# Linear-attention recurrence: state update and output in fp32, with the inverse and the output scores on block diagonals

## The chip, the cores and the metric

The kernel runs on one NeuronCore of a Trainium2 chip. The metric is the device time of one execution in microseconds; the number that counts is the median over several executions. In the profile PE is TensorE's matmul side and PEld its weight loads, DVE is VectorE, ACT is ScalarE, POOL is GpSimd and SP is SyncE, which issues most DMAs.

## The reference

Three stages follow each other: a delta-rule attention, a mixture of experts with one expert for each token, and a gated MLP. The change touches the first stage alone:

```python
# batch 4, heads 8, sequence 768, head size 48, all float32
k_n = k / (norm(k, axis=-1) + 1e-6)
state = zeros((B, H, D, D))
for t in range(S):
    y[:, :, t] = q_t @ state
    v_old = state.T @ k_t
    state = state + beta_t * outer(k_t, v_t - v_old)
x = y.transpose(0, 2, 1, 3).reshape(B * S, H * D)     # 3072 tokens x 384
x = moe(x)      # gate by argmax, 8 experts, relu(x @ w1) @ w2
x = mlp(x)      # (sigmoid(x @ w_gate) * (x @ w_val)) @ w_out
```

## The kernel before

**Stages.** Attention fills about the first 380 us of the span, the experts the next 200 and the MLP the rest. Only attention has recurrence, and only attention is changed.

**Tiling.** The sequence is cut into 24 chunks of 32 tokens (a "step" `s`). A step has 8 heads x 4 batches = 32 independent small problems. Batch `b` owns the partitions `quad(b)` = 32b to 32b+31 of each token-major tile, and its 48 state rows sit on one half of the partitions (`rows(b)`). So nearly each matmul of the loop is a small one, issued 32 times over (h, b); a matmul in fp32 shows as two MATMUL records with two weight loads in the trace, one in fp16 as one.

**One step of the main loop.** `KS` = K x state (32 fp32 matmuls). `W` = values minus `KS` (DVE). `Y` starts with Q x state (32 fp32). `U` = T x `W` (32 fp32), where T (`XTS`) is the inverse of a unit triangular 32x32 matrix per (h, b). ACT and DVE then split `U` into a high and a low fp16 half, `UH`. The state `Sps` grows in PSUM by K-transposed x U: three passes of 32 fp16 matmuls (high x high, low x high, high x low: `PASS`), with `KHG` the fp16 halves of K scaled by its inverse lengths. ACT copies the state to `SH` for the next step. `Y` gets P x U, again three passes of 32 fp16 matmuls with `PHL`, the masked scores K x Q in fp16 halves. Between these stand, on the PE, three 128x128 transposes of the step before (`XTP`), the gate's logits (`GL`) and the products K x [K, Q] of the chunk eleven steps ahead (`GP`, 24 of 32 before the state update and 8 at the step's end, in steps 1 to 12).

**Work beside it.** ACT scales the raw K of the next pair of chunks (`kh_mul`: 8 small activations a step) and makes the high halves; POOL makes the low halves (`kh_split_lo`, `p_split_lo`), scales and masks P (`p_split`), scales V (`v_mul`) and half of the triangular matrices (`scale`). DVE forms T column by column for a group of four chunks (`inv_ops`: pairs of multiply into `tmp` and add into `X`, then one transpose into `XTS`), several steps ahead; `Filler` deals these out in pieces of a fixed modelled length (`TA`, `TB`) between the step's own DVE work.

**What sets the order.** Each engine has a `Queue` that issues strictly in program order, so that an instruction that waits holds all behind it on its engine. SP's queue holds the loads of K and Q (`load_kq`), of K and V by token (`load_kth`, `load_v`) and the zeroing of the dispatch buffer (`zero_fill`).

Of the kernel before, what the change touches and what calls it, by code (L numbers as in the profile page):

```python
# [31 lines left out]
SIG, KSC = 1024.0, 64.0  # L32
# [107 lines left out]
class Attention:  # L140
# [5 lines left out]
    def run(self, small, acc, zero_fill, small_loads):  # L146
# [17 lines left out]
        rnt = cp.tile([128, NG, 32], F32, name="rnt")  # L164
# [79 lines left out]
        def p_evac(s):  # L244
            u, s2 = divmod(s, 2)
            ps = PP.pop(s)
            for h in range(8):
                A.activation(out=PM[u][:, 8 * s2 + h], in_=ps[:, h, 0:32], func=AF.Copy, scale=rnt[:, 0, 8 * s + h : 8 * s + h + 1])

        def gp_evac(s):  # L250

            ps = GPS.pop(s)
            g, s4 = divmod(s, 4)
            if s4 == 0 and g > 0:
                GPM[g] = [ep.tile([128, 32, 32], F32, tag=n, name=n, bufs=b) for n, b in (("G", 2), ("P", 2))]
            A.copy(out=GPM[g][0][:, 8 * s4 : 8 * s4 + 8], in_=ps[:, :, 0:32])
            return A.copy(out=GPM[g][1][:, 8 * s4 : 8 * s4 + 8], in_=ps[:, :, 32:64]).ins


        PMS = {}  # L260

        def p_split(u):
            g, i = divmod(u, 2)
            if g:
                pm = GPM[g][1][:, 16 * i : 16 * i + 16]
                G.tensor_tensor(out=pm, in0=pm, in1=rnt[:, g, 16 * i : 16 * i + 16].unsqueeze(2).to_broadcast([128, 16, 32]), op=ALU.mult)
            else:
                pm = PM.pop(u)
            G.tensor_tensor(out=pm, in0=pm, in1=mask.unsqueeze(1).to_broadcast([128, 16, 32]), op=ALU.mult)
            PHL[u] = wk.tile([128, 2, 16, 32], F16, tag="PHL", name="PHL", bufs=4)  # L270
            PMS[u] = pm

        def p_split_hi(u):
            A.copy(out=PHL[u][:, 0], in_=PMS[u])

        def p_split_lo(u):
            G.tensor_tensor(out=PHL[u][:, 1], in0=PMS.pop(u), in1=PHL[u][:, 0], op=ALU.subtract)

        def kh_mul(u, half=None):
            r = rnt[:, u // 2].rearrange("p (s h) -> p s h", s=4)  # L280
            for i in (range(2) if half is None else (half,)):
                kt = KTOK[u][:, i]
                if u == 0 or KA:
                    for h in range(8):
                        A.activation(out=kt[:, :, h], in_=kt[:, :, h], func=AF.Copy, scale=r[:, 2 * (u % 2) + i, h : h + 1])
                    continue
                G.tensor_tensor(out=kt, in0=kt, in1=r[:, 2 * (u % 2) + i].unsqueeze(1).to_broadcast([128, 48, 8]), op=ALU.mult)

        by_head = lambda x: x.rearrange("p d h -> p h d")

        def kh_split_hi(u):
            KH = wk.tile([128, 2, 2, 8, 48], F16, tag="KH", name="KH", bufs=2)
            for s in range(2):
                A.copy(out=KH[:, s, 0], in_=by_head(KTOK[u][:, s]))
            KHG[u] = KH

        def kh_split_lo(u):
            KH, src = KHG[u], KTOK.pop(u)
            for s in range(2):
                G.tensor_tensor(out=KH[:, s, 1], in0=by_head(src[:, s]), in1=KH[:, s, 0], op=ALU.subtract)  # L300


        def prep(g):
# [4 lines left out]
            R = R0 if g < 2 else R2  # L308
# [5 lines left out]
            def scale(E, j0, j1, i0):  # L314
                L = Lt[:, j0:j1, i0:]
                E.tensor_tensor(out=L, in0=L, in1=x[:, j0:j1].unsqueeze(2).to_broadcast([128, j1 - j0, 32 - i0]), op=ALU.mult)
                E.tensor_tensor(out=L, in0=L, in1=nbr[:, g, i0:].unsqueeze(1).to_broadcast([128, j1 - j0, 32 - i0]), op=ALU.mult)
# [26 lines left out]
        others = []  # L344
# [7 lines left out]
        def inv_ops(g, share=32):  # L352
# [53 lines left out]
            def last(F):  # L406
# [4 lines left out]
                F.done = g  # L411
                if g == 0:
# [15 lines left out]
        def x_evac(s, Yp):  # L428
# [3 lines left out]
            A.activation(out=XG[s][:, 0:384], in_=fl(Yp), func=AF.Copy, scale=1.0 / SIG)  # L432
# [10 lines left out]
        def gate_l(s, mm=None):  # L443
# [140 lines left out]
        GPM[0] = [ep.tile([128, 32, 32], F32, tag="G", name="G", bufs=2)]  # L584
# [8 lines left out]
        G.tensor_copy(out=lt, in_=small["tri"])  # L593
        for ops in prep(0):
# [46 lines left out]
        kh_mul(1)  # L641
        kh_split_hi(1)
# [4 lines left out]
        p_split_lo(0)  # L647
# [784 lines left out]
```

## Time and profile before

| | before |
|---|---|
| median of 3 runs | 1108.39 us (1106.78 to 1110.62) |
| the profiled execution | 1108.68 us, its span 1107.0 us |
| PE busy over the span | 983.4 us, 89% |
| DVE, ACT, POOL busy | 553.9, 386.6, 408.0 us |
| mean granted TensorE clock | 0.864 of full speed |

The span runs from the first to the last instruction; 1.7 us of the execution lie around it. [...] Matmul records overlap each other, so the time that a stream takes is read from its union, not from the length of one record. "issue" is idle time for which the profile shows no semaphore.

### The profile page before, as it was taken

To read this page: it belongs to the slowest core of one execution; us is meant where nothing else is said; L and a number is where in the kernel's file an instruction comes from. 1 tells how busy PE (TensorE), PEld (TensorE's weight loads), DVE (VectorE), ACT (ScalarE), POOL (GpSimd) and SP (SyncE) were. 2 spreads that over 40 slices of the span, in tenths; PEclk is the share of its full clock that TensorE was granted. 3 is DMA by queue.
4 is the path that set the end of the run, shared out by engine and by line. 5 is a ranking of instruction groups with operands and counts; after the bars stand their busy time and mean duration, and the time that the engine had idled before them with its cause. 6 is when DMAs were issued, how large, how long until landed. Compare 5 with 4: busy or idle time off the path is not lost. (4 is left out here: it accounts for less than half of the span.)

```text
span 1107.0 us, 34055 instructions
## 1 busy us (share of the span) xinstructions
PE 983.4 (89%) x15079; PEld 869.3 (79%) x15080; DVE 553.9 (50%) x1338; ACT 386.6 (35%) x848; POOL 408.0 (37%) x439
## 2 busy tenths in 40 slices
PE   7966677776766899999899999999999999999997
PEld 6955666665655798889788988888888888888886
DVE  5987698879842357777665355421211201210111
ACT  2642444444442244545445522221211211211111
POOL 3652455555622224445434423341231322312322
PEclk7965666566555599999999999999999999999999
DMA  8434322211132255555554222100000000000000
GB/s 214 115 119 118 90 75 76 72 51 47 46 104 61 75 175 166 168 168 159 159 148 134 76 59 72 44 29 1 1 29 1 15 15 1 29 1 1 29 1 29
DMA packets 49866, 82.16 MB, mean 74 GB/s; under 512 B 7193, under 2 KB 37154, under 8 KB 49714
## 3 DMA queue, kind: packets, MB, share of 16 engines
q1 hardware_dynamic: 46642, 70.48, 21.9%
q0 software_dynamic: 3072, 9.46, 2.3%
q8 instruction: 119, 1.95, 0.8%
q14 instruction: 33, 0.27, 0.1%
HBM read 64.13 MB, written 15.80 MB: 72 GB/s over the span
## 5 line engine op out<-in xcount | busy, mean ns | idle before, releaser
L1353 DVE TENSOR_TENSOR gf<-gf,g 128x512 f32<-128x512 f32 x72 | 49.5, 688 | 309.0 <-PE g L1345 308.5
L855 POOL TENSOR_TENSOR gsl<-gf,gsh 128x512 fp32r<-128x512 f32 x68 | 88.4, 1300 | 268.7 <-ACT gsh L854 268.7
L1352 ACT ACTIVATE gf<-g 128x512 f32<-128x512 f32 x72 | 43.0, 598 | 185.1 <-PE g L1345 182.4
L86 DVE TENSOR_TENSOR tmp<-X,Lt 128x60 f32<-128x60 f32 (+33 forms) x280 | 97.5, 374 | 2.0
L86 DVE TENSOR_TENSOR X<-X,tmp 128x60 f32<-128x60 f32 (+33 forms) x280 | 96.6, 370 | 1.2
L854 ACT CAST gsh<-gf 128x512 fp32r<-128x512 f32 x69 | 42.8, 620 | 145.2 <-DVE gf L1353 144.6
L1319 PE MATMUL o<-woh,gsl 128*128 128x384 f32 x272 | 87.2, 338 | 0.0
L1319 PE MATMUL o<-wol,gsh 128*128 128x384 f32 x272 | 86.5, 337 | 0.0
L1035 DVE SCALAR_TENSOR_TENSOR hl<-h,hh 128x460 fp32r<-128x460 f32 (+7 forms) x57 | 33.1, 581 | 61.6 <-ACT hh L1034 61.4
L994 PE MATMUL y<-hh,w2h 128*128 128x460 f32 (+6 forms) x168 | 60.9, 362 | 2.3 <-ACT hh L1034 2.2
L1345 PE MATMUL g<-yl,wgh 128*128 128x512 f32 x216 | 62.6, 395 | 0.0
L1345 PE MATMUL g<-yl,wvh 128*128 128x512 f32 x216 | 62.3, 395 | 0.0
L1319 PE MATMUL o<-woh,gsh 128*128 128x384 f32 x272 | 61.7, 337 | 0.0
L1345 PE MATMUL g<-yh,wgh 128*128 128x512 f32 x180 | 60.9, 395 | 0.0
L994 PE MATMUL y<-hh,w2l 128*128 128x460 f32 (+6 forms) x168 | 58.5, 348 | 0.0
L86 ACT ACTIVATE kth<-kth,rnt 128x48 f32<-128x48 f32 x192 | 54.7, 388 | 1.6 <-DMA kth<-in_ktok_dram 1.6
L86 PE MATMUL Y<-UH,PHL 32*32 32x48 f16 x2304 | 29.2, 201 | 28.9 <-issue 28.9
L1319 PEld LDWEIGHTS o<-woh,gsh 128*128 128x128 f32 x272 | 49.7, 188 | 5.8
L86 PE MATMUL Sps<-UH,KH 32*48 32x48 f16 x2208 | 28.3, 200 | 27.4 <-issue 16.1
L1319 PEld LDWEIGHTS o<-wol,gsh 128*128 128x128 f32 x272 | 50.6, 188 | 2.4
L1345 PE MATMUL g<-yh,wgl 128*128 128x512 f32 x180 | 51.9, 395 | 0.0
L1345 PE MATMUL g<-yh,wvh 128*128 128x512 f32 x180 | 51.7, 395 | 0.0
(318 smaller groups left out, 2331.4 us busy)
## 6 DMA issues: line engine op xcount, KB each, us to landing
w1r<-in_w_dram SPq DMA_DIRECT2D x32, 384.0 KB, 4.9
w2r<-in_w_dram SPq DMA_DIRECT2D x32, 384.0 KB, 3.6
KQ<-in_st_dram SPq DMA_DIRECT2D x40, 192.0 KB, 4.3
disp<-zrow SPq DMA_DIRECT2D x8, 772.0 KB, 7.0
kth<-in_ktok_dram SPq DMA_DIRECT2D x12, 384.0 KB, 3.6
VT<-in_vtok_dram SPq DMA_DIRECT2D x12, 384.0 KB
XG<-in_m2g_dram SPq DMA_DIRECT2D x12, 384.0 KB, 5.0
XG<-in_m2v_dram SPq DMA_DIRECT2D x12, 384.0 KB, 4.3
```

What stands on the lines that cost most here:

```text
L86: r = f(*args, **kw)
L854: (act or nc.scalar).copy(out=hi, in_=src)
L855: eng.tensor_tensor(out=lo, in0=src, in1=hi, op=ALU.subtract)
L994: self.T.matmul(out=ys[c][:, 0:n], lhsT=w2[l][:, f % 2, 128 * c : 128 * c + 128], rhs=(hh, hl)[r], start=(f == 0 and i == 0), stop=(f == 7 ...
L1035: self.V.scalar_tensor_tensor(out=hl, in0=hp[:, 0:n], scalar=0.0, in1=hh, op0=ALU.max, op1=ALU.subtract)
L1319: T.matmul(out=ops_[m][:, 0:384], lhsT=gh[l][:, 128 * m : 128 * m + 128], rhs=wo[r][:, f], start=(f == 0 and i == 0), stop=(f == 11 and i ...
L1345: T.matmul(out=ps, lhsT=gv[w][l][:, c, 128 * f : 128 * f + 128], rhs=Y[r][c], start=(i == 0 and c == 0), stop=(i == 2 and c == 2))
L1352: A.activation(out=gf, in_=gps[0], func=AF.Sigmoid)
L1353: V.tensor_tensor(out=gf, in0=gf, in1=gps[1], op=ALU.mult)
```

## The change

Lengths of K are no longer multiplied into K and P; they go into the scale of the inverse's rows (`nbr` is multiplied by the inverse length a second time), so U comes out scaled for raw K and raw P. The state update is one fp32 pass on the loaded K tile (`KTOK`), the output is 8 fp32 matmuls of 128x128, one a head, on P laid out as a block diagonal over the four batches (`PBD`); from the second group on `U` is 16 matmuls of 64x64 on T laid out as a two-block diagonal (`TBD`). DMAs of SP scatter T and P into these, whose other blocks are zeroed once. V is scaled on ACT, P is masked on DVE as it leaves PSUM (on POOL for the first 12 chunks), and the triangular matrices are scaled on DVE alone. The logits take three full matmuls instead of six halves.

```diff
+        PM = [cp.tile([128, 8, 32], F32, name=f"PM{i}") for i in range(RK)]
+        PBD = [cp.tile([128, 8, 4, 32], F32, name=f"PBD{i}") for i in range(2)]
+        TBD = [cp.tile([128, 32, 2, 32], F32, name=f"TBD{i}") for i in range(2)]
...
-            t = wk.tile([128, 2, 48, 8], F32, tag="kth", name="kth", bufs=1)
+            t = wk.tile([128, 2, 48, 8], F32, tag="kth", name="kth", bufs=3)
...
-            v = VT[s // 2][:, s % 2].rearrange("p (h e) -> p h e", h=8)
-            G.tensor_tensor(out=v, in0=v, in1=nt[:, g, 8 * s4 : 8 * s4 + 8].unsqueeze(2).to_broadcast([128, 8, 48]), op=ALU.mult)
+            for h in range(8):
+                v = VT[s // 2][:, s % 2, 48 * h : 48 * h + 48]
+                A.activation(out=v, in_=v, func=AF.Copy, scale=nt[:, g, 8 * s4 + h : 8 * s4 + h + 1])
...
+        def p_keep(s, ps):
+
+            A.copy(out=PM[s % RK], in_=ps)
+            G.tensor_tensor(out=PM[s % RK], in0=PM[s % RK], in1=mask.unsqueeze(1).to_broadcast([128, 8, 32]), op=ALU.mult)
...
+        def p_evac(s):
+            V.tensor_tensor(out=PM[s % RK], in0=GPS.pop(s)[:, :, 32:64], in1=mask.unsqueeze(1).to_broadcast([128, 8, 32]), op=ALU.mult)
+
+        def p_expand(s):
+            for b in range(4):
+                SP.dma_start(out=PBD[s % 2][quad(b), :, b], in_=PM[s % RK][quad(b)])
+
+        def t_expand(g):
+            for b in range(4):
+                SP.dma_start(out=TBD[g % 2][quad(b), :, b % 2], in_=XTS[g % 2][quad(b)])
...
-            sc = [(0.0, 0.0, lambda: scale(G, R, 32, R))]
-            if R:
-                sc.append((R / 12.0, 0.0, lambda: scale(V, 0, R, 0)))
+            sc = [(0.6, 0.0, lambda: scale(0, 16)), (0.33, GAP, lambda: scale(16, 32))]
...
-            if s2 == 0 and 0 < s < NSTEP - 2:
-                kh_split_lo(u + 1)
-            if s2 == 1 and u + 3 < NSTEP // 2:
-                p_split(u + 3)
...
+            while fresh:
+                t_expand(fresh.pop(0))
+            if not last:
+                p_expand(s + 1)
...
-                V.scalar_tensor_tensor(out=W, in0=vp, scalar=SIG * KSC, in1=KSp, op0=ALU.mult, op1=ALU.subtract)
+                W = wk.tile([128, 8, 48], F32, tag="W", name="W", bufs=1)
+                V.tensor_tensor(out=W, in0=vp, in1=KSp, op=ALU.subtract)
+                if s > 1 and s - 1 + LA < NSTEP:
+                    p_evac(s - 1 + LA)
...
+                for h in range(8):
+                    for p in range(2):
+                        r = slice(64 * p, 64 * p + 64)
+                        mm(out=Up[r, h], lhsT=TBD[g % 2][r, 8 * s4 + h].rearrange("p b i -> p (b i)"), rhs=W[r, h], start=True, stop=True)
             fil.run(TA if s else Q2)
-            A.copy(out=UH[:, 0], in_=Up)
...
-            V.tensor_tensor(out=UH[:, 1], in0=Up, in1=UH[:, 0], op=ALU.subtract)
+            A.copy(out=UF, in_=Up)
...
-                for i, (l, r) in enumerate(PASS):
-                    for h, b in hb:
-                        mm(out=Sps[b // 2][rows(b), 48 * h : 48 * h + 48], lhsT=KHG[u][quad(b), s2, l, h], rhs=UH[quad(b), r, h], start=False, stop=False)
+                for h, b in hb:
+                    mm(out=Sps[b // 2][rows(b), 48 * h : 48 * h + 48], lhsT=KTOK[u][quad(b), s2, :, h], rhs=UF[quad(b), h], start=False, stop=False)
...
-            for i, (l, r) in enumerate(PASS):
-                for h, b in hb:
-                    mm(out=Yp[quad(b), h], lhsT=PHL[u][quad(b), l, 8 * s2 + h], rhs=UH[quad(b), r, h], start=(s == 0 and h == 0 and i == 0), stop=(i == 2))
+            for h in range(8):
+                mm(out=Yp[:, h], lhsT=PBD[s % 2][:, h].rearrange("p b i -> p (b i)"), rhs=UF[:, h], start=(s == 0 and h == 0), stop=True)
```

On the PE one step of the second group reads before like this, in program order; the rows with `KH` and with `PHL` each stand 96 times, a weight load and a matmul each.

```order
L86 MATMUL KS<-SH,KQ_98 32x48 x32
L86 MATMUL Y<-SH,KQ_98 32x48 x32
L86 MATMUL U<-W,XT_106 32x48 x32
L86 MATMUL XTP<-cst,XG 128x128 x3
L86 MATMUL GP<-KQ_97 32x64 x24
L86 LDWEIGHTS KH
L86 MATMUL Sps_107<-UH,KH 48x48
L86 LDWEIGHTS PHL
L86 MATMUL Y<-UH,PHL 32x48
L86 MATMUL GL<-wgo,xt 64x16 x6
```

The same step of the changed kernel (`TBD` and `PBD` are the block diagonals, `UF` the fp32 copy of `U`; the rows of `Sps` go on in pairs to 32 in all):

```order
L85 MATMUL KS<-SH,KQ_97 32x48 x32
L85 MATMUL Y<-SH,KQ_97 32x48 x32
L85 MATMUL U<-W,TBD_119 64x48 x16
L85 MATMUL XTP<-cst,XG 128x128 x3
L85 MATMUL GP<-KQ_96 32x64 x24
L85 MATMUL Sps_122<-UF,kth 48x48 x2
L85 MATMUL Sps_123<-UF,kth 48x48 x2
L85 MATMUL Y<-UF,PBD_117 128x48 x8
L85 MATMUL GL<-wgo,xt 128x16 x3
```

The places are the same; 192 fp16 matmuls have become 32 small and 8 full-width fp32 ones, and `U` has half as many.

On ACT a step of the loop reads before like this (`kth` is the loaded K):

```order
L86 CAST UH<-U 128x384
L86 COPY xt<-XTP 128x384
L86 COPY SH<-Sps_107 128x384
L86 COPY SH<-Sps_108 128x384
L86 ACTIVATE XG<-Y 128x384
L86 COPY G<-GP 128x256
L86 COPY P<-GP 128x256
L86 ACTIVATE kth<-kth,rnt 128x48 x8
```

and after:

```order
L85 COPY UF<-U 128x384
L85 COPY xt<-XTP 128x384
L85 COPY SH<-Sps_122 128x384
L85 COPY SH<-Sps_123 128x384
L85 ACTIVATE VT<-VT,nt 128x48 x8
L85 ACTIVATE XG<-Y 128x384
L85 COPY G<-GP 128x256
```

The eight small activations now scale V instead of K, and stand ahead of the copy that frees the output's PSUM bank (`XG`).

On SP the DMAs around the second group's first step stand so in the changed kernel; before, the rows with `TBD` and `PBD` were not there.

```order
L85 DMA VT<-in_vtok_dram 128x768
L85 DMA disp<-zrow 256x1x772
L85 DMA TBD_119<-XT_121 32x32x32 x4
L85 DMA PBD_117<-PM_109 32x8x32 x4
L85 DMA kth<-in_ktok_dram 128x768
L85 DMA KQ_96<-in_st_dram 48x1024 x2
L85 DMA disp<-zrow 256x1x772
L85 DMA PBD_116<-PM_110 32x8x32 x4
```

Four DMAs a step lay out P for the next step, and four a group lay out T; the loads of K and Q stand behind them.

## Rows read from the trace of the kernel before

**Rows 1.** Busy time by stretch: us, PE, PEld, DVE, ACT, POOL, PE clock, DMA share, GB/s.
```profile
14.00:54.00 40.00, 35.78 (x983) 32.33 (x985) 38.22 (x145) 23.45 (x84) 25.16 (x45) 0.84 0.60 149
54.00:64.00 10.00, 4.10 (x228) 3.57 (x220) 9.76 (x17) 1.89 (x5) 8.25 (x9) 0.69 0.60 218
64.00:377.00 313.00, 222.81 (x9831) 191.40 (x9818) 222.95 (x682) 132.52 (x348) 135.83 (x195) 0.58 0.26 76
380.00:420.00 40.00, 39.12 (x338) 36.39 (x326) 24.84 (x76) 17.52 (x37) 13.81 (x12) 0.93 0.54 169
```

**Rows 2.** Instructions of `UH` on ACT: durations, first and last start.
```profile
L86 ACT CAST UH<-U x24: 464/479/479, 54.4 to 376.3; 128x384 f16<-128x384 f32 x24
```

**Rows 3.** PE groups, 64 to 377 us: busy us, mean ns, idle before and its cause.
```profile
L86 PE MATMUL Y<-SH,KQ 48*32 48x48 f32 x1448 | 40.0, 278 | 7.7 <-issue 7.6
L86 PE MATMUL U<-W,XT 32*32 32x48 f32 x1472 | 39.2, 275 | 12.5 <-issue 8.2 <-DVE W L86 4.1
L86 PE MATMUL KS<-SH,KQ 48*32 48x48 f32 x1472 | 38.1, 277 | 9.3 <-issue 9.3
L86 PE MATMUL GP<-KQ 48*32 48x64 f32 x768 | 29.0, 300 | 0.6 <-issue 0.5
L86 PE MATMUL Y<-UH,PHL 32*32 32x48 f16 x2194 | 27.9, 200 | 28.9 <-issue 28.9
L86 PE MATMUL Sps<-UH,KH 32*48 32x48 f16 x2112 | 26.8, 200 | 21.5 <-issue 13.7 <-DVE UH L86 7.2 <-ACT UH L86 0.6
L86 PE MATMUL XTP<-cst,XG 128*128 128x128 f32 x67 | 19.9, 432 | 0.8 <-issue 0.8
L86 PE MATMUL GL<-wgo,xt 128*64 128x16 f32 x264 | 18.2, 260 | 8.8 <-issue 8.4 <-DVE late L86 0.3
```

**Rows 4.** PE timeline of one step: start us, us, instruction, [idle before <-cause].
```profile
218.88 0.90 PE L86 MATMUL XTP<-cst,XG 128*128 128x128 f32 x3
219.71 1.65 PE L86 MATMUL GP<-KQ 48*32 48x64 f32 x48
...
223.13 0.48 PE L86 MATMUL Sps<-UH,KH 32*48 32x48 f16 x41 [1.17 <-issue]
...
226.59 0.27 PE L86 MATMUL Y<-UH,PHL 32*32 32x48 f16 x9 [2.19 <-issue]
...
228.04 1.48 PE L86 MATMUL KS<-SH,KQ 48*32 48x48 f32 x64
```

**Rows 5.** The page: instructions of each engine; instruction DMAs: packets, MB, share.
```profile
PE 983.4 (89%) x15079; PEld 869.3 (79%) x15080; DVE 553.9 (50%) x1338; ACT 386.6 (35%) x848; POOL 408.0 (37%) x439
...
q8 instruction: 119, 1.95, 0.8%
```

**Rows 6.** Timeline of the first step's end, and of DVE later.
```profile
53.45 0.88 PE L86 MATMUL U<-W,XT 32*32 32x48 f32 x64
54.40 0.48 ACT L86 CAST UH<-U 128x384 f16<-128x384 f32 x1 [4.48 <-PE U L86]
...
55.83 1.17 POOL L86 TENSOR_TENSOR PHL<-PM,PHL 128x512 f16<-128x512 f32 x1
...
55.96 1.11 DVE L86 TENSOR_TENSOR tmp<-X,Lt 128x60 f32<-128x60 f32 x1
...
62.61 0.55 DVE L86 TENSOR_TENSOR UH<-U,UH 128x384 f16<-128x384 f32 x1
...
101.61 0.22 DVE L86 TENSOR_TENSOR tmp<-X,Lt 128x60 f32<-128x60 f32 x1
```

**Rows 7.** ACT group, 64 to 377 us.
```profile
L86 ACT ACTIVATE kth<-kth,rnt 128x48 f32<-128x48 f32 x160 | 45.7, 377 | 1.6 <-DMA kth<-in_ktok_dram 1.6
```

**Rows 8.** Timeline: T of the third group, and the first `U` that reads it.
```profile
163.43 2.02 DVE L86 STREAM_TRANSPOSE XT<-X 128x1024 f32<-128x1024 f32 x1
...
172.63 0.86 PE L86 MATMUL U<-W,XT 32*32 32x48 f32 x30
```

**Rows 9.** DMA issues: KB each, us from issue to landing.
```profile
pf<-perm SPq DMA_DIRECT2D x1, 12.0 KB, 3.8
```

More of the change, by code (lines that the diff above doesn't have):

```diff
@@ L30 @@
 ROW = 386
-SIG, KSC = 1024.0, 64.0
 RS = 0.703952253
@@ L253, in gp_evac, with g_evac @@
+        def g_evac(s):
             g, s4 = divmod(s, 4)
             if s4 == 0 and g > 0:
[L255 to L300, printed above, removed]
+                GPM[g] = ep.tile([128, 32, 32], F32, tag="G", name="G", bufs=2)
@@ new lines, in g_evac, with gp_evac @@
+            A.copy(out=GPM[g][:, 8 * s4 : 8 * s4 + 8], in_=GPS[s][:, :, 0:32])
+        def gp_evac(s):
+            g_evac(s)
+            p_keep(s, GPS.pop(s)[:, :, 32:64])
+        def p_evac(s):
[6 more added lines that the diff above has]
+                SP.dma_start(out=TBD[g % 2][quad(b), :, b % 2], in_=XTS[g % 2][quad(b)])
@@ L312, in prep, with scale @@
             tr = lambda o, i, d: (d, 0.0, lambda: V.transpose(out=o, in_=i))
[L314 to L317, printed above, removed]
+            def scale(j0, j1):
+                L = Lt[:, j0:j1, j0:]
+                V.tensor_tensor(out=L, in0=L, in1=nbr[:, g, j0:].unsqueeze(1).to_broadcast([128, j1 - j0, 32 - j0]), op=ALU.mult)
             ops = [
-                (1.135, GAP, lambda: V.transpose(out=L1, in_=GPM[g][0].rearrange("p b c -> p c b"))),
+                (1.135, GAP, lambda: V.transpose(out=L1, in_=GPM[g].rearrange("p b c -> p c b"))),
                 (0.085, GAP, lambda: V.tensor_scalar_max(out=x, in0=L1[:, 0:1024:33], scalar1=1e-36)),
@@ L411, in last @@
                 F.done = g
+                if g:
+                    fresh.append(g)
                 if g == 0:
@@ L431, in x_evac @@
             XG[s] = XGP[s // 2][:, s % 2]
-            A.activation(out=XG[s][:, 0:384], in_=fl(Yp), func=AF.Copy, scale=1.0 / SIG)
+            A.activation(out=XG[s][:, 0:384], in_=fl(Yp), func=AF.Copy, scale=1.0)
         def gate_t(s, tp=T.transpose):
@@ L449, in gate_l @@
             for c in range(3):
-                for p in range(2):
-                    r = slice(64 * p, 64 * p + 64)
-                    mm(out=GL(g)[r, 16 * s4 : 16 * s4 + 16], lhsT=xt[:, c, r], rhs=wgo[:, c], start=(c == 0), stop=(c == 2))
+                mm(out=GL(g)[:, 16 * s4 : 16 * s4 + 16], lhsT=xt[:, c], rhs=wgo[:, c], start=(c == 0), stop=(c == 2))
         GT, GE = {}, {}
@@ L593, in run @@
         G.tensor_copy(out=lt, in_=small["tri"])
+        zap(G, PBD[0])
+        zap(G, PBD[1])
         for ops in prep(0):
@@ L616, in run @@
             f()
-        p_evac(0)
+        p_keep(0, PP.pop(0)[:, :, 0:32])
         gp_evac(4)
-        p_evac(1)
+        p_keep(1, PP.pop(1)[:, :, 0:32])
         gp_evac(5)
@@ L651, in run @@
         gp_evac(10)
-        kh_split_lo(1)
+        zap(G, TBD[1], 2)
         v_mul(1)
-        p_split(1)
-        W = wk.tile([128, 8, 48], F32, tag="W", name="W", bufs=1)
-        V.tensor_scalar_mul(out=W, in0=VT[0][:, 0].rearrange("p (h e) -> p h e", h=8), scalar1=SIG * KSC)
         ops, sc1 = prep(1)
@@ L728, in run @@
                     mm(out=Uf[:, 384:512], lhsT=zl, rhs=zl, start=True, stop=True)
[L729 to L736 removed]
+            if g == 0:
+                for h, b in hb:
+                    mm(out=Up[quad(b), h], lhsT=XTS[0][quad(b), 8 * s4 + h], rhs=W[quad(b), h], start=True, stop=True)
+            else:
+                for h in range(8):
+                    for p in range(2):
+                        r = slice(64 * p, 64 * p + 64)
+                        mm(out=Up[r, h], lhsT=TBD[g % 2][r, 8 * s4 + h].rearrange("p b i -> p (b i)"), rhs=W[r, h], start=True, stop=True)
+            fil.run(TA if s else Q2)
+            A.copy(out=UF, in_=Up)
             beside(s, "U", engines, Sps[1])
@@ L792, in run @@
                     v1 = fil.add(gate_v1(g - 1), WG)
-            if s2 == 1 and u + 3 < NSTEP // 2:
-                p_split_hi(u + 3)
-                p_split_lo(u + 3)
             if more and s:
                 gp_mm(s + LA, H8[GS:], mm)
-                gp_evac(s + LA)
+                g_evac(s + LA)
             if s == 0:
-                kh_mul(2, 0)
-                p_split(2)
                 v_mul(2)
-            elif half and s4 != 3:
-                kh_mul(u + 2, s2)
-                if s2:
-                    kh_split_hi(u + 2)
             if s2 == 1 and half:
@@ L818, in run @@
             share_rows(NR)
-            if s4 == 3 and half and s >= KL:
-                kh_mul(u + 2, s2)
-                kh_split_hi(u + 2)
             beside(s, "end", engines)
             fil.run((TB if s + 1 + LA < NSTEP else TC) if s else TB0)
-            if s4 == 3 and half and s < KL:
-                kh_mul(u + 2, s2)
-                kh_split_hi(u + 2)
             if s4 == 3 and g + 1 < NG:
```

53 lines of the change are left out of this document (15 added, 38 removed).

## The prediction

> **What bounds the kernel now.** I read the page first, then busy time by stretch, then the PE's groups in the attention loop, then single steps on the timeline. From 380 us on the PE is all but full [rows 1] and nothing there is changed, so the answer lies in the attention. The 24 starts of the copy of `U` run from 54.4 to 376.3 us [rows 2]: 23 steps of 14.0 us. In 64 to 377 us the PE is busy for 222.8 of 313.0 us, 71% [rows 1]. The idle times ahead of its groups add up to 90.1 us: 77.4 "issue", 7.2 on DVE for the low half of `U`, 0.6 on ACT for the high half, 4.1 on DVE for `W`, 0.8 the rest [rows 3]. So the loop is neither a dependence chain nor DVE, though DVE is as busy as the PE (222.95 us): it is the PE in program order, with holes for which no semaphore is to blame.
>
> What are the holes? More than half, 28.9 and 13.7 us, lie ahead of the fp16 streams of `Y` and `Sps` [rows 3], and one step shows them in the middle of such a stream: 1.17 us within `Sps`, 2.19 us within `Y` [rows 4]. Those streams go through instructions fastest: 27.9 us for 2194 matmuls is 12.7 ns each, against 26.6 ns in `U` and 25.9 ns in `KS` [rows 3]. And the queue of instruction DMAs moved 1.95 MB [rows 5]: divided by the PE's 30,159 matmuls and weight loads that is 65 bytes each, in 119 packets of some 253. I take this queue to feed the PE, and the holes to be waits for its next packet. That is inferred; the profile has no row that says so.
>
> **The change, part by part.** All sums are for the profiled execution (1108.68 us, span 1107.0, 1.7 around it, which stay). It is within 0.3 us of the median.
>
> *Waits for instructions.* A step with `GP` has 64 records each of `KS`, `Y`, `U` and `GP`, 96 of `Sps`, 96 of the output, 3 of `XTP`, 12 of `GL`: 463 with as many weight loads. After, `U` has 32, `Sps` 64, the output 16, `GL` 6: 313, or 68%. In proportion 52 of the 77 us stay. But the two fast streams are gone, and every stream left takes 26 ns a matmul or more, half the old rate; if the feed keeps up with that, nearly none stays. I take 20 us: gain **57**, between 26 and 77.
>
> *The low half.* The state update no longer waits for DVE: 7.8 us in the loop [rows 3]. In the first step `U` is copied at 54.40 and the low half comes only at 62.61, since DVE has other work ahead of it [rows 6]; the PE is busy for 4.1 of these 10 us [rows 1]. With `GP` to fill the gap I count 5 us there. Gain **13**, between 5 and 15.
>
> *State update.* 64 records at 26.6 ns are 1.70 us, in place of 96 at 12.7, 1.22 us: 0.48 us in 23 steps, loss **11**.
>
> *Output.* Sixteen records of 128x128 by 48 columns in place of 1.22 us. No row shows this shape. From below: four small fp32 matmuls share the array and come 26.6 ns apart, so one alone takes 4 x 26.6 = 106 ns; 16 make 1.70 us, +0.48 a step. From above: a 128x128 transpose costs 19.9 us / 67 = 297 ns, 4.75 us, +3.5 a step. Between, `GL` loads 64 weight columns for 16 moving ones at 18.2 us / 264 = 69 ns; with twice the columns 139 ns [all rows 3]. I take that, being a stream with weight loads of nearly this kind: 2.2 us, loss **24** over 24 steps, between 12 and 85.
>
> [...]
>
> *`U` and the logits.* Two blocks instead of four share the array, for half as many matmuls: 32 x 53 = 1.7 us as now. Six `GL` of twice the columns: as now. Zero.
>
> *Laying out T and P.* The DMAs of P are not on the path: four are issued at the start of a step, behind a wait for the output of the step before, and have until the end of the next, over 10 us. Behind that wait in SP's queue stand `kth`, K and Q, which already wait for matmuls of the same step, later in it. T is tighter. Its 4 DMAs make 4096 pieces; the nearest row, 3072 pieces of 4 bytes, lands in 3.8 us [rows 9], so about 5.1 here. T of the third group is ready at 165.45 and read at 172.63 [rows 8], 7.2 us later; a step 2 us shorter leaves 5. I count 1.2 us for each of five groups: loss **6**, between 0 and 20. `U` waits there, and behind it on the PE everything.
>
> *Work moved among ACT, POOL and DVE.* ACT's eight activations a step change their subject (377 ns each [rows 7], 3.0 us); they now stand ahead of the copy that frees `Y`'s bank. After the state update ACT needs three copies of 0.48 us, each the size of that of `U` [rows 2], and the 3.0: 4.5 us, and the PE has output, logits and `KS` for 2.2 + 0.8 + 1.7 = 4.7 before it wants the bank. Just covered; without cover it costs up to 0.5 us a step. POOL loses nearly all its large operations. While one ran, a DVE multiply of 128x60 took 1.11 us, and 0.22 without [rows 6]. DVE gets the mask 12 times and the scaling of five groups, loses 23 low halves of 0.55 us, and should become lighter on balance. This is worth little where DVE does not set the pace: gain **2**, in the first inverse before the loop, where DVE is busy for 38.2 of 40 us [rows 1].
>
> *Clock.* The granted clock was 0.58 in the loop at a PE share of 71%, 0.84 at 89%, 0.93 at 98% [rows 1]. With 35 us of work more and 65 us of holes less, the share rises to some 90%. [...] For a rise to 0.65, 14% of some 258 us of PE work shrinks by about 40%: gain **15**, from 0 to 40.
>
> Sum: -57 - 13 + 11 + 24 + 6 - 2 - 15 = -46; 1108.7 - 46 = **1063 us**, steps of about 12.1 us.
>
> **The rivals.**
>
> *Slower: the full-width output.* If each of its matmuls costs what a transpose does, 297 ns, the loss there is 85 instead of 24, and the PE's share is made of such waits, so that the clock brings nothing: 1063 + 61 + 15 = 1139. Without the clock's 15 us it decides from 2.3 us more a step than now (55 us in all, what the other terms gain), 16 x 0.22 us. For it: it is the only fp32 stream with 128 weight columns besides the transposes. Against it: three transposes in 0.90 us [rows 4] carry the length of one record, 432 ns, so the step between them is nearer 235 ns, and they have 128 moving columns, not 48.
>
> *The holes stay.* If the PE waits for packets in proportion to its instructions whatever their pace, 52 of 77 us stay: +32, and with no clock gained +15: 1110, no change. For it: `KS`, `U` and `GL` wait too, 25.9 us together [rows 3], though they are slow streams. Against: they follow the fast ones and may pay for these.
>
> *T comes late.* If its DMAs take 12 us to land, or stand behind the zeroing of the dispatch buffer, `U` waits some 7 us at five groups, 35 instead of 6: 1092.
>
> *The clock opens.* At 0.75 instead of 0.65 in the loop the PE's work shrinks by another 20 us or so: 1042. For it: the loop's share would be that of 14 to 54 us, which got 0.84. Against: that stretch has dummy matmuls put in on purpose. [...]
>
> **How the numbers follow.** The main case 0.50 (1063, by itself 1050 to 1080), the clock opens 0.15, T late 0.13, holes stay 0.12, output slow 0.10. 1035 to 1108 holds the first three and half of the fourth. Within 0.3%, 3.3 us, is about what a measurement of this kernel can tell from no change. Faster takes the first three and some of the fourth, 0.83; the same 0.05; slower the fifth and a little of the fourth, 0.12.
>
> **What would show it.** In the profile after: "issue" ahead of the PE's groups falls from 77 to about 20 us, and the instruction queue from 119 packets to about 92 (24 steps by some 290 instructions less, over 253). No wait of `Sps` for DVE is left. The output's 16 records take about 2.2 us, the state update 1.7. The clock in the loop is 0.6 to 0.7. `U` waits for the T DMAs by a few us in all, or not. DVE's 128x60 multiplies are near 0.22 us throughout. From 380 us on everything is as before, only earlier. I am wrong if the holes are no instruction waits, if the full-width matmuls come over 0.2 us apart, or if DVE, 71% busy and in strict order, becomes what `W` waits for once the PE is faster.

## The result, and the profile after

The changed kernel takes 1075.9 us (median; 1068.3 to 1079.7), the kernel before 1107.6 us beside it: a ratio of 0.970, 95% interval 0.964 to 0.976. The forecast of 1063 us had the direction and held the time in its range; it is 13 us low. The execution that was profiled is the shortest of the changed kernel's, 1068.3 us (span 1066.6), so the steps of the sum are 5 us off when profile is set against profile.

Page of the changed kernel, instructions of each engine and instruction DMAs (answers to [rows 5]), then busy time by stretch, in the columns of [rows 1]; the third stretch stops at 330 us, where the loop now ends:

```profile
PE 1027.5 (96%) x11639; PEld 925.3 (87%) x11640; DVE 477.3 (45%) x1329; ACT 344.2 (32%) x772; POOL 311.0 (29%) x363
...
q8 instruction: 93, 1.52, 0.6%
```

```profile
14.00:54.00 40.00, 36.63 (x924) 32.20 (x923) 38.21 (x144) 10.32 (x35) 23.40 (x50) 0.92 0.76 212
54.00:64.00 10.00, 10.00 (x412) 9.40 (x408) 8.97 (x35) 4.83 (x15) 1.29 (x2) 1.00 0.09 16
64.00:330.00 266.00, 253.70 (x6302) 235.09 (x6296) 149.72 (x655) 99.24 (x309) 45.28 (x120) 0.66 0.44 108
```

The PE's share of the loop has gone from 71% [rows 1] to 95%, POOL's from 43% to 17%; 26 instruction packets are gone. The copies of `U` on ACT (in [rows 2] `UH`) bound the loop:

```profile
L85 ACT COPY UF<-U x24: 480/480/483, 55.5 to 331.5; 128x384 f32<-128x384 f32 x24
```

23 steps in 276.0 us, 12.0 each, where [rows 2] had 321.9 us. That is all of the gain and a little more: the loop gives 45.9 us, the first `U` comes 1.1 us later, and from the last `U` to the end of the span it is 735.1 us where it was 730.7. The PE's groups, 64 to 330 us (answers to [rows 3], which reached to 377 us):

```profile
L85 PE MATMUL Y<-UF,PBD 128*128 128x48 f32 x352 | 58.9, 334 | 0.0
L85 PE MATMUL Sps<-UF,kth 32*48 32x48 f32 x1408 | 38.9, 273 | 1.7 <-issue 1.4 <-ACT UF L85 0.3
L85 PE MATMUL U<-W,TBD 64*64 64x48 f32 x618 | 36.2, 283 | 7.2 <-DMA TBD<-XT 5.1 <-DVE W L85 1.4 <-issue 0.5
L85 PE MATMUL Y<-SH,KQ 48*32 48x48 f32 x1384 | 32.5, 267 | 0.0
L85 PE MATMUL KS<-SH,KQ 48*32 48x48 f32 x1408 | 32.3, 262 | 0.8 <-issue 0.7
...
L85 PE MATMUL GL<-wgo,xt 128*128 128x16 f32 x132 | 24.4, 315 | 0.4 <-DVE late L85 0.4
...
L85 PE MATMUL U<-W,XT 32*32 32x48 f32 x136 | 3.4, 248 | 2.1 <-issue 2.1
```

"issue" is down to 4.9 us over all groups. (Busy time over count, not the mean duration, is the distance from one record to the next: records overlap.) The output is now the largest group, 58.9 us / 352 = 167 ns a record of 334 ns.

### The profile page after: what moved, and what is told of

Same layout as the page of the kernel before. It is cut to its first block, busy times and chain, and to the rows that moved or that the text cites. A ratio compares the mean times of both kernels' runs of the same rounds, so it can differ in the third digit from the quotient of the medians.

```text
span 1066.6 us, 27205 instructions
## 1 busy us (share of the span) xinstructions
PE 1027.5 (96%) x11639; PEld 925.3 (87%) x11640; DVE 477.3 (45%) x1329; ACT 344.2 (32%) x772; POOL 311.0 (29%) x363
## 5 line engine op out<-in xcount | busy, mean ns | idle before, releaser
L85 DVE TENSOR_TENSOR tmp<-X,Lt 128x84 f32<-128x84 f32 (+36 forms) x278 | 72.1, 286 | 1.8
L85 DVE TENSOR_TENSOR X<-X,tmp 128x84 f32<-128x84 f32 (+36 forms) x278 | 71.2, 282 | 1.1
L85 PE MATMUL Y<-UF,PBD 128*128 128x48 f32 x384 | 64.5, 335 | 0.0
L85 PEld LDWEIGHTS Y<-UF,PBD 128*128 128x128 f32 x384 | 61.1, 250 | 1.6
L1288 PE MATMUL g<-yh,wgh 128*128 128x512 f32 x180 | 60.9, 395 | 0.0
L978 DVE SCALAR_TENSOR_TENSOR hl<-h,hh 128x460 fp32r<-128x460 f32 (+7 forms) x57 | 33.1, 581 | 61.7 <-ACT hh L977 61.5
L85 POOL COPY XG<-g_sc 128x2 f32<-128x2 f32 x24 | 6.8, 284 | 154.8 <-DVE g_sc L85 139.5
```

The source lines that it names most:

```text
L85: r = f(*args, **kw)
L978: self.V.scalar_tensor_tensor(out=hl, in0=hp[:, 0:n], scalar=0.0, in1=hh, op0=ALU.max, op1=ALU.subtract)
L1288: T.matmul(out=ps, lhsT=gv[w][l][:, c, 128 * f : 128 * f + 128], rhs=Y[r][c], start=(i == 0 and c == 0), stop=(i == 2 and c == 2))
```

## The experiments

One table for all. Time is the median, and the ratio is to the kernel before run beside each (its medians: 1106.4 to 1113.2 us, and 1107.6 beside the changed kernel), so compare runs by their ratios. The rest is from one profile each: us a step (first to last copy of `U`, over 23), and of the stretch 64 to 330 us the PE's matmuls and busy us, "issue" idle summed over its groups, and granted clock. The profiled execution is the shortest of the changed kernel (1068.3 us) and the longest of e9 (1075.1) and e12 (1070.3), so their steps do not stand for their medians.

| kernel | us | ratio [95%] | step | matmuls | PE busy | issue | clock |
|---|---|---|---|---|---|---|---|
| before | 1107.6 | 1 | 14.0 | 8475 | 189.2 | 63.7 | 0.60 |
| changed | 1075.9 | 0.970 [0.964, 0.976] | 12.0 | 6302 | 253.7 | 4.9 | 0.66 |
| e1_out_small | 1068.5 | 0.961 [0.957, 0.965] | 11.5 | 7810 | 238.0 | 19.8 | 0.67 |
| e2_u_small | 1077.2 | 0.966 [0.961, 0.971] | 12.4 | 6797 | 246.6 | 16.5 | 0.66 |
| e3_all_small | 1073.4 | 0.965 [0.960, 0.969] | 11.8 | 8362 | 223.6 | 40.0 | 0.69 |
| e4_before_one_pass | 1064.1 | 0.957 [0.952, 0.963] | 11.7 | 6894 | 182.5 | 26.1 | 0.60 |
| e5_out_small_start | 1055.1 | 0.952 [0.949, 0.955] | 11.3 | 7689 | 230.5 | 26.2 | 0.74 |
| e6_more_instr | 1111.7 | 1.003 [1.001, 1.005] | 13.8 | 6581 | 262.8 | 2.4 | 0.59 |
| e7_pool_back | 1108.2 | 1.001 [0.999, 1.004] | 13.5 | 5651 | 220.0 | 2.0 | 0.66 |
| e8_out_logits_small | 1059.5 | 0.955 [0.952, 0.959] | 11.5 | 7725 | 221.5 | 36.0 | 0.74 |
| e9_out_half | 1062.7 | 0.961 [0.957, 0.965] | 11.9 | 6977 | 247.0 | 11.2 | 0.66 |
| e10_small_more_instr | 1076.1 | 0.973 [0.970, 0.977] | 12.1 | 8051 | 228.1 | 34.4 | 0.69 |
| e11_more_instr_quads | 1093.5 | 0.989 [0.984, 0.993] | 12.9 | 6581 | 256.7 | 6.8 | 0.60 |
| e12_first_u_small | 1062.2 | 0.957 [0.953, 0.960] | 11.6 | 7818 | 232.4 | 31.2 | 0.69 |

(The expectations of e9 to e11 count gaps of matmuls and weight loads together: 10.8 us in the changed kernel where this sum has 4.9, 26.5 in e5 where it has 26.2.)

The theory: the holes of before are the PE waiting for instructions, so a kernel with fewer and slower ones wins, and block diagonals pay by needing fewer. The rivals: the PE's own work sets the time; VectorE's relief does.

**The block diagonals undone, one by one.** In e1 the output goes back to 32 small fp32 matmuls:

```diff
-            for h in range(8):
-                mm(out=Yp[:, h], lhsT=PBD[s % 2][:, h]..., rhs=UF[:, h], ...)
+            for h, b in hb:
+                mm(out=Yp[quad(b), h], lhsT=PM[s % RK][quad(b), h], rhs=UF[quad(b), h], ...)
```

> The changed kernel with the output P x U as 32 small fp32 matmuls a step (as the state update), without the block diagonal of P and its DMAs. In the loop of the changed kernel a full-width output record cost 62.5 us / 368 = 170 ns, 2.7 us a step; the state update's 64 small records 38.9 us / 22 = 1.77 us. Theory A (the holes came from the fp16 streams running through instructions faster than they are fed; fp32 streams do not): no holes come back, a step loses 0.95 us, 24 steps 23 us: ratio to the kernel before about 0.95. Theory B (the feed has a mean limit: the kernel before drew 19,649 instructions in 313 us, a packet of 253 in 4.0 us, and cannot draw faster): a step of 722 instructions is 2.85 packets, 11.5 us at least, so at most 0.5 us a step is gained and issue waits return; ratio 0.96 to 0.97.

In e2 `U` reads T from `XTS` in every group, as in the first, and TBD and its DMAs are gone:

```diff
-            if g == 0:
                 for h, b in hb:
-                    mm(out=Up[quad(b), h], lhsT=XTS[0][quad(b), 8 * s4 + h], ...)
-            else: ... TBD ...
+                    mm(out=Up[quad(b), h], lhsT=XTS[g % 2][quad(b), 8 * s4 + h], ...)
```

> The changed kernel with U as 32 small fp32 matmuls on T as the transpose leaves it, in all groups; no block diagonal of T and no DMAs for it. Theory A: 64 records at 26 ns in place of 32 at 37.4 us / 640 = 58 ns, 0.2 us a step, and the waits for T at five group starts (5.1 us shown on DMA, and some 2 us within each first U of a group) go: 8 to 12 us faster than the changed kernel, ratio about 0.96. Rival: the T waits are hidden by something later (W waits for DVE, which makes T), and the step is the same: ratio 0.97.

In e3 both, and the logits in halves, so that the fp32 passes are left of the change, with the work that it moved among ACT, POOL and DVE:

```diff
-                mm(out=GL(g)[:, ...], lhsT=xt[:, c], rhs=wgo[:, c], ...)
+                for p in range(2):
+                    r = slice(64 * p, 64 * p + 64)
+                    mm(out=GL(g)[r, ...], lhsT=xt[:, c, r], rhs=wgo[:, c], ...)
```

> Both at once, and the logits in six halves as before: no block diagonals, no DMAs for them, fp32 throughout. A step has 798 instructions, 3.15 packets of 253. Theory A: output 0.95, U 0.2, logits 0.3 us a step and the T waits: 24 x 1.45 + 8 = 43 us faster than the changed kernel, ratio 0.93. Theory B: 3.15 packets x 4.0 us = 12.7 us a step at least, slower than the changed kernel by 0.5 us a step, ratio 0.98, with issue waits of tens of us.

The output's 64 small records cost 29.8 us / 1472 = 20 ns each in e1, 1.3 us a step against 2.7. The step gained 0.5 of these 1.4 us, since "issue" went from 4.9 to 19.8 us. In e2 the T waits go and issue waits come: no gain, as its rival had it, though not for the rival's reason (waits on `W` for DVE stayed at 1.6 us). In e3 the PE is busy 30 us less than in the changed kernel and waits 35 us more on "issue"; its 0.965 lies between the forecasts of theory A (0.93) and B (0.98). e3 also bears on the theory's first half. Busy time by stretch of before and of e3:

```profile
64.00:330.00 266.00, 189.17 (x8475) 163.36 (x8462) 209.49 (x638) 119.44 (x321) 125.04 (x179) 0.60 0.27 77
```

```profile
64.00:330.00 266.00, 223.63 (x8362) 195.96 (x8362) 156.60 (x682) 100.97 (x320) 44.76 (x121) 0.69 0.31 89
```

Two programs of quite different work a matmul run off almost the same number in 266 us, 8475 and 8362, and these are the two with most "issue"; in both the instruction queue moved 66 packets in this stretch. So the fp32 passes with the moved work bring what the whole change brings (0.965 and 0.970, the intervals overlap): the block diagonals together are worth nothing, and that of the output costs. e3 also begins its loop late, as e1 does (below): its first `U` is copied at 65.0 us. What the passes bring without the moved work no run of the changed kernel shows; e7 below and e4 bear on it.

**The fp16 streams alone, from the other side.** e4 is the kernel before with one pass of three in the state update and the output:

```diff
-                for i, (l, r) in enumerate(PASS):
+                for i, (l, r) in enumerate(PASS[:1]):
```

> The kernel before with only the first of the three fp16 passes (high x high) in the state update and in the output; the low halves are still made by DVE and POOL, and read by nobody. This leaves out the small correction terms of both sums. It keeps all of the work of ACT, DVE and POOL and takes 128 matmuls a step from the PE, 1.6 us of its work. Theory A (holes are waits for instructions that fast fp16 streams outrun): most of the 77 us of issue waits go as well, the loop falls by 1.6 + 2 to 3 us a step, to 10 to 10.5 us, unless DVE, slowed by POOL, becomes the bound at about 11; ratio 0.92 to 0.94. Rival C (the gain of the change came from DVE and POOL being relieved): only the 1.6 us of PE work can go, most of it into waits for DVE; ratio 0.97 to 1.0.

With 128 matmuls a step fewer "issue" falls from 63.7 to 26.1 us, and another wait appears. Waits of the PE in e4, 64 to 330 us: us in total, times, longest:

```profile
PE U L86 <- DVE W L86: 55.6, 16, 9.5
PE Y L86 <- issue: 10.7, 11, 2.6
```

VectorE, busy for 228.5 of the 266 us, is what `U` now waits for. Both forecasts missed: 0.957 lies between theory A's 0.92 to 0.94 and rival C's 0.97 to 1.0, since most of the "issue" went, as A had it, and DVE took up a part of it, as C had it.

**Why e1's loop began late.** Its first `U` was copied at 65.3 us instead of 55.5 in the changed kernel. Without the DMA of P ahead of the loop, which waits for POOL, the zeroing of the dispatch buffer behind it on SP's queue starts at once, and from 14 us on the DMA engines are full. e1's stretch, and its PE waits from 28 to 54 us:

```profile
14.00:30.00 16.00, 11.09 (x408) 9.50 (x407) 15.21 (x61) 3.74 (x14) 7.78 (x20) 0.71 1.01 260
```

```profile
PE GP L85 <- issue: 5.1, 2, 4.0
PE P L85 <- issue: 2.9, 1, 2.9
```

The changed kernel's DMA share in this stretch is 0.54. Packets of the instruction queue start at 18.2, 25.8 and 34.3 us in e1, and the PE had run dry at 25.5 and 33.0; in the changed kernel they start at 17.8, 22.0, 26.2 and 30.1. The early zeroing is not enough by itself: the kernel before starts it as early (17.1 us, e1 17.0), shows a share of 0.98 in this stretch, and copies its first `U` at 54.4. But there SP's queue waits for POOL behind the second such DMA, 12.9 us (23.8 to 36.7), and the share is 0.33 from 30 to 42 us, where e1 has 1.02. e5 is e1 with that one DMA put back, its target read by nothing:

```diff
+        PB0 = cp.tile([128, 8, 4, 32], F32, name="PB0")
         gp(7)
+        for b in range(4):
+            SP.dma_start(out=PB0[quad(b), :, b], in_=PM[0][quad(b)])
         gp_evac(6)
```

> The changed kernel with the output as 32 small fp32 matmuls a step (the run e1_out_small) and with the work ahead of the loop held in the changed kernel's order: P of step 0 alone still goes into a block diagonal by four DMAs, which nothing reads, so that the zero fill that stands behind them on SP's queue waits for P again. In e1_out_small the first U came at 63.2 us instead of 54.1 us, with the DMA engines full of the zero fill from 14 to 42 us and TensorE waiting for instructions in between. If that collision is the cause, the first U is back near 54 us, the steps keep e1's 11.5 us, and the time is about 9 us under e1's 1068.5: 1059 us. Rival: the zero fill then runs into the first steps, or another thing sets the start, and the time stays at 1065 to 1070 us.

The first copy of `U` moved to 59.2 us, so 6.1 of the 9.8 us came back (e8, with the same work ahead of the loop, has 55.3, and e12 60.9; what moves it by these 5 us is open), and the time to 1055.1 us, 1.9% under the changed kernel by their ratios to before (0.952 / 0.970): the best kernel here. Part of its gain over e1 is not the start but a shorter step, 11.3 us for 11.5, at a clock of 0.74 for 0.67.

**e5 varied.** e8 puts the logits in halves (e3's lines); e9 leaves heads 0 to 3 on block diagonals (`for h in range(4)` wide, `hb[16:]` small; made from the changed kernel); e10 adds instructions and hardly any work:

```diff
+            for i in range(8):
+                for b in range(4):
+                    mm(out=Uf[quad(b), 384 + 4 * i : 388 + 4 * i], lhsT=zl[quad(b), 0:32], rhs=zl[quad(b), 0:4], ...)
```

> e5_out_small_start with the logits in halves again (12 records of about 60 ns a step for 6 of 187 ns: 0.72 us for 1.12). TensorE's work falls by 0.4 us a step, 9 us in all; 12 instructions a step more. Theory of the instruction feed: half of it comes back as waits: 4 us under e5, about 1055 us. Rival, work alone: 9 us under e5, about 1050 us.

> The changed kernel with heads 0 to 3 of the output on block diagonals (full width, 170 ns a record) and heads 4 to 7 as small matmuls (20 ns a record): between the changed kernel (12.0 us a step, waits for instructions 10.8 us in 64 to 330 us) and e5_out_small_start (11.3 us a step, 26.5 us of such waits). TensorE's output work is 2.0 us a step for 2.7 and 1.3. If work alone counted, or both in proportion, it would lie half-way: 11.7 us a step, 1065 us. If the rate at which instructions arrive sets a floor under e5, as its waits say, the half kernel is nearer to e5 than to the changed kernel: its waits for instructions fall towards 15 us, 11.3 to 11.5 us a step, 1053 to 1059 us.

> e5_out_small_start with 32 tiny fp16 matmuls a step behind the output (32x32 weights, 4 columns, over the four quarters of the array in turn, into columns that nothing reads): 64 instructions more a step, for which e6_more_instr's 29 ns each is avoided if the quarters work side by side (12.5 ns as in the fp16 streams of the kernel before: 0.4 us a step). Work alone: 9 us more than e5, waits for instructions as there (26 us in 64 to 330 us) or less: 1064 us. Feed at its limit: the waits grow as well, to 32 us or more, and the time goes to 1068 to 1080 us.

e8: 9 us less work, 10 us more "issue", no gain: the waits take it all back, more than either theory had. e9: half-way between its two neighbours, 1062.7 us (0.961 between 0.952 and 0.970); no hard floor shows, and the forecast of less than 1059 missed. e10: +21 us for dummies whose own time is 10.7 us / 689 = 15.5 ns, 0.5 us a step. Its holes stand ahead of other groups than e5's, where the first two of these rows had 3.8 and 1.1 us of "issue" (and `KS` 10.3, in e10 5.7):

```profile
L85 PE MATMUL Y<-SH,KQ 48*32 48x48 f32 x1408 | 34.4, 260 | 8.0 <-issue 8.0
...
L85 PE MATMUL Y<-UF,PM 32*32 32x48 f32 x1352 | 25.5, 231 | 9.1 <-issue 9.1
...
L85 PE MATMUL U<-zl 32*32 32x4 f16 x689 | 10.7, 165 | 6.6 <-issue 6.5
```

Per step "issue" went from 26.2 / 266 x 11.3 = 1.1 us to 1.6 us; the sum is what counts, since 31 of e10's 32 holes over 0.3 us end 1.2 to 1.7 us after a packet of the instruction queue has landed, whichever group is next. Instructions with hardly any work raised "issue" here from 26.2 to 34.4 us.

**More instructions in the changed kernel.** e6 puts 48 dummies behind the output, all on the same weights and columns (`mm(out=Uf[0:32, 384:388], lhsT=zl[0:32, 0:32], rhs=zl[0:32, 0:4])`); e11 has e10's 32, over the four quarters.

> The changed kernel with 48 more matmuls a step (fp16, 32x32 weights, 4 columns, into columns of U's PSUM bank that nothing reads) right behind the output: 96 more instructions on TensorE a step, as many as e1_out_small has more, at hardly any work. Theory that TensorE's instructions arrive at a limited rate and that block diagonals pay by needing fewer of them: waits for instructions in 64 to 330 us rise from about 4 us to some 20 us, as in e1_out_small, beside at most 13 ns a matmul of their own (14 us in all): 1095 to 1110 us. Rival, TensorE's work alone counts: the waits stay under 8 us, and the time rises by the matmuls' own 8 to 14 us: 1084 to 1090 us.

> The changed kernel with the same 32 tiny matmuls a step as e10_small_more_instr: it needs 568 instructions a step in 12.0 us, some 47 a us where the kernel before ran 64 a us with 77 us of waits, so the feed has room. Theory: the time rises by the matmuls' own 0.4 us a step alone, 9 us, to 1085 us, and waits for instructions stay under 14 us. Rival (any added instruction makes holes, whatever the rate): waits of 20 us and more, 1095 us or above.

e6 missed both ways: no holes, yet +36 us. Its dummies on one quarter came 26.8 us / 912 = 29 ns apart, 1.4 us a step, and so slowed the stream that should have outrun the supply; it says nothing on the supply. In e11 they cost 7.5 us / 640 = 12 ns, 0.4 us a step, with 6.8 us of "issue": holes stay away, as the theory had it. But its time of 1085 us was missed by 8: the step grew by 0.9. The PE is busy 12.4 us a step (256.7 / 266 x 12.9) for 11.4 in the changed kernel; 0.6 us of that is the same work taking longer, at a clock of 0.60 for 0.66.

**GpSimd's work put back.** e7 is the changed kernel with four multiplications of an unread tile a step:

```diff
+            if s:
+                for _ in range(4):
+                    G.tensor_tensor(out=SCR, in0=SCR, in1=mask.unsqueeze(1).to_broadcast([128, 16, 32]), op=ALU.mult)
```

> The changed kernel with GpSimd's tensor work put back in amount: four multiplications of a scratch tile of 128x512 with the mask at the head of every step, about 4.6 us a step (the kernel before has some 4 us a step more on GpSimd than the changed one). Nothing reads the tile. Theory: the gain is TensorE's (fewer and longer instructions), and VectorE, slowed by GpSimd, has slack: VectorE's busy time in 64 to 330 us rises from 150 to 180 us or more, and the time by 0 to 8 us. Rival: the relief of VectorE is a good part of the gain: U's matmuls wait for W or T comes late, and the time rises by 15 to 30 us, to 1090 to 1106 us.

The rival won, and by more than its 1106 us: the whole gain is gone. DVE's multiplies of 128x60 in the changed kernel and then in e7 (busy us, mean ns), 64 to 330 us:

```profile
L85 DVE TENSOR_TENSOR X<-X,tmp 128x60 f32<-128x60 f32 x16 | 3.3, 220 | 0.2
L85 DVE TENSOR_TENSOR tmp<-X,Lt 128x60 f32<-128x60 f32 x16 | 3.2, 218 | 0.3
```

```profile
L85 DVE TENSOR_TENSOR X<-X,tmp 128x60 f32<-128x60 f32 x16 | 8.6, 549 | 0.2
L85 DVE TENSOR_TENSOR tmp<-X,Lt 128x60 f32<-128x60 f32 x16 | 6.6, 424 | 0.3
```

and the PE's waits in e7:

```profile
PE U L85 <- DVE W L85: 24.7, 8, 9.2
PE U L85 <- DMA TBD<-XT: 8.2, 6, 2.5
PE U L85 <- POOL X L85: 6.4, 1, 6.4
```

VectorE is busy for 221.3 of 266 us instead of 149.7, and `U` waits. The load was on the heavy side: POOL was busy for 149.6 us in this stretch, before for 125.0; so 32 us is more than the true price, which no run shows.

**T's wait taken away.** e12 is e5 with the first `U` of each group straight from T (`if g == 0 or s4 == 0:`), so that T's DMAs have a step to land.

> e5_out_small_start, with U of the first step of each group of four taken straight from T as 32 small matmuls, and from the block diagonals in the other three steps, so that T's DMAs (7.2 to 8.4 us from issue to landing in e5) have a whole step to land. In e5 TensorE stood 5.5 us for these DMAs in 64 to 330 us, and in the changed kernel the first U of a group took 3.8 to 4.5 us where the others take some 2 (three of the five groups). If these waits set the path: 8 to 12 us less than e5, 1043 to 1047 us. Rival, as in e2_u_small: what the waits give back is taken by waits for instructions (64 more in one step of four): 1053 to 1058 us.

The wait for `TBD` is gone, 5.5 us in e5 and none here, "issue" grew from 26.2 to 31.2 us, and the clock was 0.69. No gain, if anything a loss (0.957 for e5's 0.952): as in e2, the rival's reason held, though 1062 us is above its 1053 to 1058.

## Why the prediction was right, and where it was not

**Waits for instructions** (-57 taken): 77.4 us [rows 3] became 4.9, so -72, near the far bound of 77. The reason stands up: "issue" rises with the matmuls run off per us (changed 6302, e9 6977, e5 7689, e10 8051, e3 8362, before 8475 in 266 us: 4.9, 11.2, 26.2, 34.4, 40.0, 63.7 us; e1, e2, e8 and e12 lie up to some 10 us beside this row, and e4, which still has fp16 streams, 16 us above it), and e10 raised it with instructions of hardly any work. Queue packets came to 93 where 92 were named. That the holes are waits for packets was inferred in the prediction; the trace of the kernel before shows it, since it has the start and the duration of each packet of the instruction queue. Five holes of "issue", the first two those of [rows 4] (the packet's landing is its start plus its duration; the place is the count of the PE's matmuls and weight loads up to the hole's end):

| ahead of | hole, us | ends | last packet landed | later by, us | place |
|---|---|---|---|---|---|
| `Sps` | 1.17 | 223.13 | 221.77 | 1.36 | 12970 |
| `Y` | 2.19 | 226.59 | 225.20 | 1.39 | 13226 = 12970 + 256 |
| `GL` | 1.78 | 251.84 | 250.38 | 1.46 | 15018 = 12970 + 8 x 256 |
| `Y` | 0.79 | 255.85 | 254.41 | 1.44 | 15274 = 12970 + 9 x 256 |
| `Sps` | 0.67 | 259.86 | 258.43 | 1.43 | 15530 = 12970 + 10 x 256 |

A packet has 16,384 bytes, and the 66 packets of 64 to 330 us face 16,937 matmuls and weight loads, 257 each. Of the 50 holes of "issue" over 0.3 us in that stretch, 47 (61.5 of 62.7 us) end 1.2 to 1.7 us after a packet has landed, while only 12% of the stretch lies so behind a landing. In e5 it is 23 of 23, in e10 31 of 32. The packets start 3.8 us apart in the median in the kernel before and in e3, 5.0 in the changed kernel.

**The low half** (-13): no wait of `Sps` for DVE is left, and in 54 to 64 us the PE is busy for 10.0 us instead of 4.1 [rows 1]. The 2 us from the first inverse did not come: the first `U` is 1.1 us later.

**State update** (+11): 38.9 us / 1408 x 64 = 1.77 us a step for the 1.70 of the sum.

**Output** (+24): the loss that was mis-sized most, by 11 us (only the waits, by 15, were further off). It took 139 ns a record from `GL`'s twice 69; measured were 167, 2.7 us a step instead of 2.2: +35. The price is not one number. Stretch and output group of the changed kernel at a granted clock of 1.00 and of 0.50:

```profile
192.00:212.00 20.00, 19.68 (x622) 18.39 (x621) 14.12 (x58) 9.73 (x29) 6.66 (x24) 1.00 0.48 96
...
288.00:330.00 42.00, 38.93 (x766) 35.73 (x767) 10.46 (x37) 14.06 (x38) 5.38 (x8) 0.50 0.30 79
```

```profile
L85 PE MATMUL Y<-UF,PBD 128*128 128x48 f32 x32 | 4.0, 277 | 0.0
...
L85 PE MATMUL Y<-UF,PBD 128*128 128x48 f32 x48 | 10.9, 415 | 0.0
```

4.0 / 32 = 125 ns at 1.00 and 10.9 / 48 = 227 ns at 0.50. The 139 ns taken lie between the two, and the 106 ns counted from below are under both.

**Logits** ("as now", 0): wrong for the same reason: 6 records of 24.4 us / 132 = 185 ns are 1.1 us a step for 0.8, +6. I had doubled the columns and halved the count at one price per column. **`U`** came to 1.8 us for 1.7, +3.

**T** (+6): 5.1 us of waits, near the number, but not as 1.2 us for each of five groups: three waited 1.4 to 2.1 us, two not. The four DMAs of the first two groups took 6.9 us from the first issue to the last landing, those of the last 11.5; 5.1 had been taken. One step that was hit, timeline of the PE:

```profile
100.93 0.44 PE L85 MATMUL U<-W,TBD 64*64 64x48 f32 x2
102.91 1.91 PE L85 MATMUL U<-W,TBD 64*64 64x48 f32 x30 [1.53 <-DMA TBD<-XT]
```

Taking it away gave nothing (e2, e12).

**Work moved** (-2, "worth little where DVE does not set the pace"): the number was harmless, the sentence wrong. POOL's relief is the cover under which the rest of the gain lies: with a load like the old one back, DVE sets the pace (e7, where `U` waits 24.7 us for DVE's `W`), and with the PE alone made faster it does so too (e4, 55.6 us). I had named that as a way to be wrong, and gave the cover no price. What the cover is worth stays open: e7's load was too heavy to say.

**Clock** (-15, 0.58 to 0.65): 0.66 came, and `KS` and `Y` on K, Q cost 23 ns a record for 27. No run shows the 14% and the 40% of which the 15 us are made; the traces show a granted clock of 0.50 in 93 and of 1.00 in 15 of the 133 slices of 2 us from 64 to 330 us before, of 0.50 in 78 and of 1.00 in 34 in the changed kernel, and the output's 227 and 125 ns at these two. But the reason failed, and so the number is luck: over the kernels the clock does not follow the PE's busy share. e6 is busy for 99% of the stretch at 0.59, e5 for 87% at 0.74, and the changed kernel shows 0.50 at 93% and 1.00 at 98% (the two stretches above). What the granted clock goes by is left open here.

**In sum.** Idle time of the PE fell from 90.1 / 313 x 14.0 = 4.0 us a step to 12.3 / 266 x 12.0 = 0.55, its work rose from 222.8 / 313 x 14.0 = 10.0 [rows 1] to 253.7 / 266 x 12.0 = 11.45. Over 23 steps that is -80 and +34, the loop's -46. The forecast had -64 (57 + 13 - 6) and +20 (11 + 24 - 15): both too small by some 15 us, and so the step of 12.1 us came out: the direction and the main mechanism were right; that the two errors cancelled is luck. (The terms above, taken record by record and with what `KS`, `Y` and `XTP` gained, add up to some +44 of work; why that is more than the +34 is not shown.) With 1.1 us at the start and 4.4 us behind the loop, neither foreseen, it is the -40.4 of the spans. The 4.4 are lost in the first 20 us after the last `U`, where the PE is full in both kernels and the granted clock is 0.58 in the changed one and 0.77 before: the `cn` matmul, early in the experts, starts 19.1 us after that copy of `U`, before 14.5. The 8 us from there to the median lie between executions of the changed kernel (mean clock over the span 0.90 in the profiled one, 0.88 to 0.89 in the other three), not in a step of the sum.

## What to carry to other kernels

Where an engine is idle with no semaphore to blame, count its instructions per microsecond, and see whether its holes end a fixed time after a packet of the instruction queue: here, in the kernel before, 47 of 50 ended 1.2 to 1.7 us after a landing. "issue" came to 2.0 to 6.8 us of 266 at 21.2 to 24.7 matmuls (with their weight loads) a us (changed, e6, e7, e11) and to 11.2 to 63.7 us at 25.6 to 31.9 (all others), where work saved was partly or wholly paid back (e1 kept 0.5 of 1.4 us a step, e8 none of its 9 us). Before fewer, wider matmuls are bought for that reason, price the wide one at each granted clock that the trace shows, here 125 ns at 1.00 and 227 at 0.50: 2.7 us against 1.3 for the output was more than the instructions were worth. And when one engine is sped up, ask for the price of each relief that covers it, and see what else a removed DMA was holding back on its queue.

## What was not expected of the hardware

- In the kernel before, 47 of 50 holes without a semaphore ended 1.2 to 1.7 us after an instruction packet of 16,384 bytes had landed, and those 47 stand a multiple of 256 of the PE's instructions apart, to within one.
- With four multiplications of 128x512 a step put on GpSimd (e7), VectorE's of 128x60 took 424 ns instead of 218 and 549 instead of 220 on average, and the whole gain of the change was gone (a ratio of 1.001 for 0.970).
- Tiny matmuls on one quarter of the array with the same columns came 29 ns apart, the same spread over four quarters 12 ns (e6, e11).
- 0.4 us of added matmuls a step cost 0.9 us (e11); the granted clock was 0.60 instead of 0.66 with the PE no less busy (97% and 95%).
- With the DMA engines full (share 1.01 and 1.02 from 14 to 42 us in e1), instruction packets started 7.6 and 8.5 us apart, and TensorE stood up to 4.0 us at a time; in the changed kernel, at 0.54 from 14 to 30 us, they started about 4 us apart.
